# Attention with a top-1 mixture of experts on one core: second operands of VectorE in PSUM, late weight splits on ScalarE and VectorE, early loads regrouped

## The chip, the core and the metric

The kernel runs on one core of one Trainium2 chip. Time is device time in microseconds (us) of one execution; lower is better. The kernel before took 995.2 us (median of three runs, 991.33 to 996.54). A core has five engines that run beside each other and wait for each other by semaphores: TensorE (PE, its weight loads PEld), VectorE (DVE), ScalarE (ACT), GpSimd (POOL) and SyncE (SP, which here only issues transfers). Each works through its own instructions in order, so an instruction that waits holds all that stands behind it on its engine.

## What is computed

```python
scores = scale * q @ k.T                      # 8 batches x 8 heads, 576 x 576, head size 64
thresh = max(scores, -1) - tau                # tau = 0.02
scores = where(scores >= thresh, scores, -1e9)
attn   = exp(scores - max); attn /= attn.sum(-1) + 1e-9
x      = (attn @ v), heads side by side       # 4608 tokens x 512
logits = x @ w_gate + modality_bias[modality_id]
e      = argmax(logits)                       # one of 8 experts per token
gate_w = softmax(logits)[e]
out    = gate_w * (relu(x @ w1[e]) @ w2[e])   # 512 -> 1024 -> 512, all in fp32
```

## The kernel before

Attention goes pair of heads by pair of heads (32 pairs), each pair in 9 steps of 128 query rows, 288 steps in all. A step is: `qk` (PE, four matmuls of 288 columns into two PSUM banks, L827), `soft_a` (DVE row maximum L836 and threshold L838, ACT exponential L842), `soft_b` (DVE: keep what passes the threshold, with row sums, L854), `tr` (PE transposes of the probabilities L880, ACT copies them out of PSUM, L883; a remainder of 64 columns is copied by POOL or ACT, L867 and L869). Once per pair `tr_rem` and `pv` multiply with the values (L761), `x_out` turns the result (DVE, L943) and SP stores it to `xs` in device memory. For accuracy every fp32 matmul is done as three (or two) passes over high and low parts in fp32r; the "splits" that make these parts are a cast (high) and a subtraction (low).

Keys and queries of the next pair come by SP, are turned (`turn_rows`, pairs 1 to 8, by PE; `turn`, later pairs, by DVE), split by POOL (`stack`, L727 and L729) and moved between partitions by SP (`move`).

After every fourth pair a batch is complete: `gate` computes the logits, `route` (DVE, L996 to L1029) picks each token's expert and its place in a table, POOL scatters the rows into it (L1033). `pick` then chooses an expert with enough waiting tokens for a "side slot". A slot is up to 512 tokens of one expert: POOL gathers them (L1160), they are scaled by the softmax sums (L1182, `xt`), turned by PE (L1187) and split (L1191 ACT, L1192 DVE), the expert's 16 weight chunks of 128x512 are loaded by SP and split (`wsplit`, L1219 to L1223), then the first layer (`l1`, L1239, with `hh` by ACT L1251 and `hl` by DVE L1253) and the second (`l2`, L1271, results by L1279 and L1283, scattered to `out` by POOL, L1290) run on PE. Eight side slots run beside attention and just behind it; the last of them (nb = 8) can only start when all batches are routed. Then `pick_rest` (DVE, 17 short pieces on one partition, L1060 to L1126) chooses the three slots of the tail, of 512, 512 and 320 tokens, whose tiles have a `t` in front of their names (`traw`, `tw1l`, `tw2l`, `txg`).

In the side slots POOL scales `xn` and makes both parts of every weight chunk; in the tail DVE scales `xn`, ACT makes the high parts, DVE the low part of w1, POOL that of w2.

The order in which each engine's instructions stand is made while the kernel is built: every piece of work is an `op` with an engine, an assumed duration, what it reads and writes, and a due time; `Plan.order` plays these against each other with assumed latencies (`LAT`, `NEXT`, `OVER`, and `LAND` for transfers) and writes out each engine's list. A string `SHIFTS` moves every due time by a fixed amount of its own. The four single PSUM banks (`bk`) during attention, eight behind it (`bk` and `pm`), are given out by the same planner: a `Group` holds one bank from its first use to its last.

Of the kernel before, what the change touches and what calls it, by code (L numbers as in the profile page):

```python
# [77 lines left out]
class Plan:  # L78
# [4 lines left out]
    LAND = (0.2, 1.05, 1.7, 4.5)  # L83
# [62 lines left out]
    def order(self, banks, late):  # L146
# [54 lines left out]
        def begin(e, t):  # L201
# [51 lines left out]
            for j in o.succ:  # L253
                x = ops[j]
                same = x.eng == o.eng and o.dma is None
                x.soon = max(x.soon, fin + (self.NEXT if same else self.LAT).get(o.eng, 0.0 if same else 0.04))
                x.left -= 1
                if not x.left and x.hot:
                    coming.add(j)
# [7 lines left out]
        while heap:  # L267
            t = heap[0][0]
            while heap and heap[0][0] <= t + 1e-9:
# [9 lines left out]
                else:  # L279
# [10 lines left out]
                    for j in o.succ:  # L290
                        s = ops[j]
                        same = s.eng == o.eng and o.dma is None
                        s.ready = max(s.ready, t + (self.NEXT if same else self.LAT).get(o.eng, 0.0 if same else 0.04))
# [52 lines left out]
def tile_attn_moe(  # L346
# [138 lines left out]

    def load(out, in_, rd=(), wr=(), us=1.0, due=None, eng="SP"):
        q_ = {"SP": nc.sync, "ACT": nc.scalar, "POOL": nc.gpsimd}[eng]
        op(eng, 0.6, lambda: q_.dma_start(out=out, in_=in_), rd, list(wr) or [out], dma=us, due=due)
# [15 lines left out]
    vr2 = tiles(glob, 2, [P, 2, D], F32, "vr")  # L504
# [8 lines left out]
    pos2 = tiles(glob, 2, [P, NT + 1, NE], F32, "pos")  # L513
# [44 lines left out]
    def begin():  # L558
        op("DVE", 0.1, lambda: nc.vector.memset(warm, 0.0), wr=[warm])
        op("DVE", 0.1, lambda: nc.vector.memset(zero, 0.0), wr=[zero])  # L560
        def part(z, s, x, eng):
            load(first[z][s].t.rearrange("p (c x d) -> p c x d", c=NC, x=2)[:, :, x, :],
                 (k, q)[z][0, s, 0:SA, :].rearrange("(c p) d -> p c d", c=NC), wr=[(first[z][s], x)], us=0.4, eng=eng)
# [54 lines left out]
    def late_constants():  # L618
# [15 lines left out]
        mid_i = bi.t[:, 0:2 * B * NT].bitcast(I32).rearrange("p (b t two) -> p b t two", b=B, t=NT)  # L634
        mid_v = mid.bitcast(I32).rearrange("(b s two) -> b s two", s=S, two=2)
# [7 lines left out]
        def f():  # L643
            nc.vector.tensor_copy(out=mid_f[:, 1, :], in_=mid_i.rearrange("p b t two -> p (b t) two")[:, :, 0])
            nc.vector.tensor_scalar(out=mid_f[:, 0, :], in0=mid_f[:, 1, :], scalar1=0.0, scalar2=None,
                                    op0=ALU.is_equal)
        op("DVE", 0.8, f, [(bi, b) for b in range(B + 1)], [bf])
        for m, (t, key) in enumerate(((bias_t, bias_t), (bias_u, bu))):
            op("DVE", 0.45, lambda m=m, t=t: nc.vector.tensor_tensor(
                out=t, in0=mb_b[:, m:m + 1, :].to_broadcast(shp),  # L650
                in1=mid_f[:, m, :].unsqueeze(2).to_broadcast(shp), op=ALU.mult), [bx, bf], [key])
        op("DVE", 0.45, lambda: nc.vector.tensor_tensor(out=bias_t, in0=bias_t, in1=bias_u, op=ALU.add),
           [bias_t, bu], [bias_t])
        for b, xs_ in ((bx, [bx]), (bi, [(bi, b) for b in range(B + 1)])):
# [22 lines left out]
    def load_rows(p):  # L677
# [225 lines left out]
    def pv(p):  # L903
        vt, vr = vm2[p % 2], vr2[p % 2]
# [34 lines left out]
    def x_out(p):  # L939
# [6 lines left out]
        for a in range(KC):  # L946
# [3 lines left out]
                 src.rearrange("i k p r -> i k (p r)"), rd=[src], wr=[("xs", b, h, a)], us=0.6)  # L950
# [36 lines left out]
    def counted(nb):  # L987
        return pos2[(nb - 1) % 2][:, NT, :] if nb else creg

    def route(b):  # L990
# [3 lines left out]

        def f1():
            V.tensor_reduce(out=lt, in_=lg.rearrange("p c h e -> p c e h"), axis=AX.X, op=ALU.add)  # L996
            V.tensor_reduce(out=mx, in_=lt, axis=AX.X, op=ALU.max)
            V.tensor_tensor(out=lt, in0=lt, in1=mx.unsqueeze(2).to_broadcast(shp_t), op=ALU.subtract)

        def f2():  # L1000
            V.scalar_tensor_tensor(out=fe, in0=lt, scalar=0.0, in1=iota_m.unsqueeze(1).to_broadcast(shp_t),
                                   op0=ALU.is_ge, op1=ALU.mult)
            V.tensor_reduce(out=mn, in_=fe, axis=AX.X, op=ALU.min)
            V.tensor_tensor(out=oh[:, 0:NT, :], in0=iota_x, in1=mn.unsqueeze(2).to_broadcast(shp_t), op=ALU.is_equal)
        op("DVE", 1.35, f1, [lg], [lt, mx])
# [12 lines left out]
        def f4():  # L1018
            rkv = g.t[:, 0:(NT + 1) * NE].rearrange("p (t e) -> p t e", e=NE)
            V.tensor_tensor(out=pos, in0=rkv, in1=counted(b).unsqueeze(1).to_broadcast([P, NT + 1, NE]), op=ALU.add)  # L1020
            V.tensor_tensor(out=pos[:, 0:NT, :], in0=pos[:, 0:NT, :], in1=oh[:, 0:NT, :], op=ALU.mult)
            V.tensor_reduce(out=posf, in_=pos[:, 0:NT, :], axis=AX.X, op=ALU.add)
            V.memset(posf[0:P - R, NC:NT], float(TROWS))
            V.tensor_copy(out=posi, in_=posf)
        op("DVE", 1.0, f4, [g, counted(b), oh], [pos, posf, posi])
# [537 lines left out]
```

## Time and profile before

| | |
|---|---|
| runs | 991.33, 995.2, 996.54 us |
| the profiled execution | 1002.75 us, span from first to last instruction 1000.9 us |
| PE busy | 961.2 us (96%) |
| DVE busy | 747.2 us (75%) |
| ACT busy | 614.3 us (61%) |
| POOL busy | 593.8 us (59%) |
| mean granted TensorE clock | 0.988 |
| last attention step (L854) begins | 757.6 us |

Busy time is from the start of an instruction to its end, so it holds the time in which an instruction stands and waits for a resource inside the engine. PE's matmuls overlap, and their ends are modelled. [...]

### The profile page before, as it was taken

How to read it: one execution, taken by the hardware profiler on the slowest of the kernel's cores; microseconds unless marked ns; L12 is line 12 of the kernel's file. 1: busy time of each engine (PE TensorE's matmuls, PEld its weight loads, DVE VectorE, ACT ScalarE, POOL GpSimd, SP SyncE). 2: the span in 40 equal slices, each digit the busy share in tenths (PEclk: the TensorE clock that was granted, in tenths of full speed). 3: DMA queues.
4: the chain of work that ended last, by engine and by line, in shares of the span. 5: the costliest groups of instructions: out<-in, count | busy, mean ns of one | idle time of the engine just before them, and what ended most of it. 6: DMA issues, size and time to landing. Idle time of an engine off the chain costs nothing.

```text
span 1000.9 us, 19578 instructions
## 1 busy us (share of the span) xinstructions
PE 961.2 (96%) x6304; PEld 768.8 (77%) x6304; DVE 747.2 (75%) x1792; ACT 614.3 (61%) x1256; POOL 593.8 (59%) x746
## 2 busy tenths in 40 slices
PE   7999999989999999999899999999999989899997
PEld 6776677768787877778789778877887866688886
DVE  6898888878788979878878888879785574625242
ACT  6777678667767776767577668766764233143431
POOL 3533686487378645737667575538964879823241
PEclk9999999999999999999999999999999989999999
DMA  7888989888879996897679786778753376333410
GB/s 162 167 192 183 196 189 191 169 204 185 182 140 194 191 193 128 185 183 167 148 158 200 178 171 147 179 142 186 190 136 87 97 199 200 116 104 103 142 63 28
DMA packets 310448, 159.58 MB, mean 159 GB/s; under 512 B 235902, under 2 KB 281982, under 8 KB 308416
## 3 DMA queue, kind: packets, MB, share of 16 engines
q1 hardware_dynamic: 301024, 138.64, 64.3%
q0 software_dynamic: 7200, 19.07, 6.2%
q8 instruction: 52, 0.85, 0.4%
q10 hardware_dynamic: 2112, 0.52, 0.2%
q14 instruction: 60, 0.49, 0.2%
HBM read 85.98 MB, written 20.73 MB: 107 GB/s over the span
## 4 chain that ended last, share of the span: by engine, by line
PE 48%; DVE 5%; issue 3%; POOL 2%; ACT 1%; another core or an unknown queue 0%; POOLq 0%; ACTq 0%; DVEq 0%
PE bk L1239 11%; PE bk L1271 11%; PE bk L761 7%; PE s L827 7%; PE bk L880 5%; PE pm L1271 3%; PE pm L1239 1%; PE bk L1187 1%; DVE pr L854 1%; DVE nm L836 1%; DVE xn L1182 1%; DVE le L1090 1%; PE bk L893 1%; POOL out_dram L1290 0%; PE bk L961 0%
## 5 line engine op out<-in xcount | busy, mean ns | idle before, releaser
L842 ACT ACTIVATE e<-s,nm 128x576 f32<-128x576 f32 x288 | 213.9, 746 | 73.6 <-DVE nm L836 67.9
L854 DVE SCALAR_TENSOR_TENSOR pr<-s,nm,e 128x576 f32<-128x576 f32 x288 | 231.3, 812 | 28.8 <-ACT e L842 10.2
L836 DVE TENSOR_REDUCE nm<-s 128x1 f32<-128x576 f32 x288 | 214.8, 749 | 30.7 <-PE s L827 25.3
L827 PE MATMUL s<-km,q 128*128 128x288 f32 x1024 | 190.9, 313 | 7.0 <-DVE pr L854 5.0
L883 ACT COPY ptm<-bk 128x512 f32<-128x512 f32 x256 | 146.3, 592 | 45.3 <-PE bk L880 37.0
L827 PEld LDWEIGHTS s<-km,q 128*128 128x128 f32 x1024 | 147.5, 189 | 34.4 <-DVE pr L854 14.0
L880 PE MATMUL bk<-ident,pr 128*128 128x128 f32 x1152 | 166.4, 275 | 1.4 <-DVE hl L1253 1.4
L880 PEld LDWEIGHTS bk<-ident,pr 128*128 128x128 f32 x1152 | 136.6, 141 | 19.1 <-issue 2.9
L761 PE MATMUL bk<-ptm,v_m 128*64 128x256 f32 (+1 forms) x1024 | 139.7, 417 | 2.3 <-ACT ptr L900 2.3
L761 PEld LDWEIGHTS bk<-ptm,v_m 128*64 128x64 f32 x1024 | 69.2, 138 | 53.6 <-issue 11.1
L1253 DVE SCALAR_TENSOR_TENSOR hl<-bk,hh 128x512 fp32r<-128x512 f32 (+3 forms) x78 | 45.9, 591 | 64.3 <-ACT hh L1251 64.1
L1239 PE MATMUL bk<-xh,w1h 128*128 128x512 f32 (+2 forms) x240 | 89.7, 374 | 0.2
L729 POOL TENSOR_TENSOR q<-kqt,q 128x576 fp32r<-128x576 f32 x62 | 88.0, 1423 | 2.3
L1271 PE MATMUL bk<-w2h,hh 128*128 128x512 f32 x200 | 84.7, 423 | 0.0
L1239 PE MATMUL bk<-xh,w1l 128*128 128x512 f32 (+2 forms) x240 | 83.8, 349 | 0.4 <-POOL w1l L1223 0.4
L1223 POOL TENSOR_TENSOR w1l<-raw,w1h 128x512 fp32r<-128x512 f32 x64 | 82.3, 1288 | 2.9
L1239 PE MATMUL bk<-xl,w1h 128*128 128x512 f32 (+2 forms) x240 | 83.6, 348 | 0.0
L1223 POOL TENSOR_TENSOR w2l<-raw,w2h 128x512 fp32r<-128x512 f32 x64 | 81.9, 1284 | 2.2
L1271 PE MATMUL bk<-w2l,hh 128*128 128x512 f32 x200 | 79.5, 398 | 2.0 <-POOL w2l L1223 2.0
L727 POOL CAST q<-kqt 128x576 fp32r<-128x576 f32 x62 | 41.0, 668 | 65.0 <-PE s L827 36.7
L1271 PE MATMUL bk<-w2h,hl 128*128 128x512 f32 x200 | 79.1, 396 | 0.0
L1290 POOL DMA_INDIRECT out_dram<-y,tb x37 | 38.2, 1034 | 61.8 <-DVE y L1283 46.1
(226 smaller groups left out, 1784.7 us busy)
## 6 DMA issues: line engine op xcount, KB each, us to landing
raw<-in_moe_w_dram SPq DMA_DIRECT2D x128, 256.0 KB
km<-q SPq DMA_DIRECT2D x60, 288.0 KB
q<-q SPq DMA_DIRECT2D x30, 576.0 KB
nk<-km SPq DMA_DIRECT2D x97, 144.0 KB
traw<-in_moe_w_dram SPq DMA_DIRECT2D x48, 256.0 KB
xs<-xq SPq DMA_DIRECT2D x64, 144.0 KB
v_m<-in_v_dram SPq DMA_DIRECT2D x64, 128.0 KB
kq<-in_q_dram SPq DMA_DIRECT2D x46, 144.0 KB
```

Source lines behind the costliest of these rows:

```text
L729: op("POOL", 1.425, lambda s=s: nc.gpsimd.tensor_tensor(out=q2[:, 1, s], in0=kqt[:, s], in1=f32(q2[:, 0, s]), op=ALU.subtract), [kqt[:, s] ...
L761: nc.tensor.matmul(out=o, lhsT=lhsT, rhs=rhs, start=start, stop=stop, skip_group_check=True)
L827: nc.tensor.matmul(out=g.t[:, hf, 0:SH], lhsT=a, rhs=x, start=(z == 0), stop=(z == len(passes) - 1))
L836: op("DVE", 0.757, lambda: nc.vector.tensor_reduce(out=nm[:, 0, x:x + 1], in_=g.t[:, :, 0:SH], axis=AX.XY, op=ALU.max, negate=True), [g], ...
L842: op("ACT", 0.747, lambda: nc.scalar.activation(out=e, in_=g.t[:, :, 0:SH], func=AF.Exp, bias=nm[:, 0, x:x + 1]), [g, nm[:, 0, x:x + 1]], ...
L854: op("DVE", 0.826, lambda: nc.vector.scalar_tensor_tensor(out=pr.rearrange("p (a x) -> p a x", a=2), in0=g.t[:, :, 0:SH], scalar=nm[:, 1, ...
L880: op("PE", 0.44, lambda: [nc.tensor.transpose(out=g.t[:, kc * P:(kc + 1) * P], in_=pr[:, kc * P:(kc + 1) * P], identity=ident) for kc in r ...
L883: op("ACT", 0.583, lambda: nc.scalar.copy(out=o, in_=g.t.rearrange("a (k p) -> a k p", p=P)), [g], [o])
L1223: op("DVE" if d else "POOL", 0.686 if d else 1.29, lambda: (nc.vector if d else nc.gpsimd).tensor_tensor(out=lo.t, in0=raw.t, in1=f32(hi.t ...
L1239: nc.tensor.matmul(out=g.t[:, 0:WT], lhsT=a.t[:, cs], rhs=x.t[:, c, 0:WT], start=(c == 0 and y == 0), stop=(c == KC - 1 and y == 2))
L1253: op("DVE", 0.1 + 0.58 * WT / 512, lambda: nc.vector.scalar_tensor_tensor(out=hl.t[:, 0:WT], in0=g.t[:, 0:WT], scalar=0.0, in1=f32(hh.t[:, ...
L1271: nc.tensor.matmul(out=g.t, lhsT=a.t[:, ts], rhs=w.t, start=(y == 0 and i == 0), stop=(y == F2 - 1 and i == 2))
```

## The change

- `route` and `pick_rest` keep their intermediate values in a PSUM bank, so that of two tensor operands of a DVE instruction one lies in PSUM; the slots whose `xn` DVE scales get the softmax sums copied into a PSUM bank by ACT first. Some instructions are split or added for this.
- From 2 us behind the planned end of attention on (`OWN`), and in the last side slot, ACT makes the high part and DVE the low part of every weight chunk, w2 of the tail included; the last side slot's `xn` is scaled by DVE.
- Values of pairs 0 to 8 come with one transfer for both heads, four rows of device memory behind each other per partition; the keys of these pairs are laid out in the same order. The 64 remaining rows of the values of two pairs come together (`load_vr`), into one buffer of four heads in place of two buffers of two.
- The modality words come by POOL, five transfers of 4-byte words in place of nine by SP of 8-byte words, and the bias is made from them by POOL.
- The planner's assumed durations of transfers change, a wait of SP for a landing costs 0.7 more, and `SHIFTS` is another.

```diff
-    LAND = (0.2, 1.05, 1.7, 4.5)
+    LAND = (0.0, 1.0, 1.95, 4.9)
+    WAKE = 0.7
...
-        for b in range(B):
-            load(mid_i[:, b, 0:NC, :], mid_v[b, 0:SA, :].rearrange("(c p) two -> p c two", c=NC), wr=[(bi, b)], us=0.4)
-        load(mid_i[:, :, NC, :], mid_v[:, S - P:S, :].rearrange("b p two -> p b two"), wr=[(bi, B)], us=0.7)
+        for t, o in enumerate([*range(0, SA, P), S - P]):
+            load(mid_i[:, :, t], mid_v[:, o:o + P].rearrange("b p -> p b"), wr=[(bi, t)], us=0.5, eng="POOL")
...
-            nc.vector.tensor_copy(out=mid_f[:, 1, :], in_=mid_i.rearrange("p b t two -> p (b t) two")[:, :, 0])
+            nc.gpsimd.tensor_copy(out=mid_f[:, 1, :], in_=mid_i.rearrange("p b t -> p (b t)"))
...
         for s in range(2):
-            load(t[:, s], sv[s, 0:SA, :].rearrange("(c p) d -> p c d", c=NC), us=0.6)
-            load(r[s * R:(s + 1) * R], sv[:, SA:S, :].rearrange("s r d -> r s d"), us=0.2)
+            if p >= ROWS:
+                load(t[:, s], sv[s, 0:SA, :].rearrange("(c p) d -> p c d", c=NC), us=0.6)
+            elif s == 0:
+                load(t.rearrange("p s c d -> p s (c d)"), sv[:, 0:SA, :].rearrange("s (p c) d -> p s (c d)", c=NC), us=1.05)
+
+    def load_vr(p):
+        b, j = p // NPAIR, p % NPAIR
+        if p % 2 == 0:
+            for s in range(2):
+                load(vr4[s * R:(s + 1) * R], v[b, 2 * j:2 * j + 4, SA:S, :].rearrange("s r d -> r s d"), us=0.3)
...
-            V.tensor_reduce(out=mx, in_=lt, axis=AX.X, op=ALU.max)
-            V.tensor_tensor(out=lt, in0=lt, in1=mx.unsqueeze(2).to_broadcast(shp_t), op=ALU.subtract)
+            V.tensor_reduce(out=one(48), in_=lt, axis=AX.X, op=ALU.max)
+            V.tensor_tensor(out=part(64, NT), in0=lt, in1=one(48).unsqueeze(2).to_broadcast(shp_t), op=ALU.is_ge)
+            V.tensor_tensor(out=lt, in0=lt, in1=one(48).unsqueeze(2).to_broadcast(shp_t), op=ALU.subtract)
...
-        cum = fin["pool"].tile([1, 3, NE], F32, name="cum", bufs=1)
+        cum = room(3, NE)
...
+    OWN = tm(NSTEP) + 2
...
+                if xt_eng and t == 0:
+                    box["r"] = gr = Group()
+                    op("ACT", 0.25, lambda: nc.scalar.copy(
+                        out=gr.t[:, 0:TT * H].rearrange("p (t h) -> p t h", h=H), in_=tb.t[:, 0:TT, 2:TC].bitcast(F32)),
+                       late + [tb], [gr], due=plan.due - 2)
...
-                if xt_eng:
+                d = xt_eng or plan.due > OWN
+                if d:
                     op("ACT", 0.62, lambda: nc.scalar.copy(out=hi.t, in_=raw.t), late + [raw], [hi])
                 else:
                     op("POOL", 0.613, lambda: nc.gpsimd.tensor_copy(out=hi.t, in_=raw.t), [raw], [hi])
-                d = xt_eng and which == 1
                 op("DVE" if d else "POOL", 0.686 if d else 1.29, lambda: (nc.vector if d else nc.gpsimd).tensor_tensor(
                     out=lo.t, in0=raw.t, in1=f32(hi.t), op=ALU.subtract), late + [raw, hi], [lo])
...
-        for t, f in slot(z, lambda cells=cells: cells["c"], nb * S, w, rings, False, [pk_i[z]], hold=hold)(t0, span, OPEN):
+        for t, f in slot(z, lambda cells=cells: cells["c"], nb * S, w, rings, nb == B, [pk_i[z]], hold=hold)(t0, span, OPEN):
```

`part`, `one` and `room` are slices of the PSUM bank that the planner gives to `route` and to `pick_rest`.

On DVE, in the middle of `pick_rest`, there stood before (`cum`, `off`, `le` are small tiles of one partition, `hl` is the low part of a first layer's result):

```order
L1253 SCALAR_TENSOR_TENSOR hl_110<-bk_79,hh_106 128x512
L1085 TENSOR_TENSOR off<-off,ns 1x24
L1086 TENSOR_TENSOR off<-off,cum 1x24
L1090 TENSOR_TENSOR le<-ij,cum 1x88 x3
L1094 TENSOR_REDUCE ej<-le 1x33
L1098 TENSOR_SCALAR em<-ej 1x33
```

and now:

```order
L1299 SCALAR_TENSOR_TENSOR hl_110<-bk_80,hh_106 128x512
L1269 TENSOR_TENSOR w1l_90<-raw_81,w1h_87 128x512
L1115 TENSOR_TENSOR cum_t<-bk_78,tri 1x64
L1116 TENSOR_REDUCE bk_78<-cum_t 1x8
L1118 TENSOR_TENSOR off<-off,bk_78 1x24
L1120 TENSOR_TENSOR bk_78<-off,bk_78 1x24
L1124 TENSOR_TENSOR le<-ij,bk_78 1x88 x3
L1299 SCALAR_TENSOR_TENSOR hl_111<-bk_79,hh_107 128x512
```

`cum` has become a slice of a PSUM bank, and the low parts of weight chunks (`w1l`) stand between the pieces.

On POOL, where the tail's first rows are gathered (`txg`), there stood before:

```order
L1221 CAST w1h_87<-raw_84 128x512
L1223 TENSOR_TENSOR tw2l_9075<-traw_9055,tw2h_9067 128x512
L1223 TENSOR_TENSOR w1l_90<-raw_84,w1h_87 128x512
L1290 DMA out_dram<-y_118,tb_121 4608x512
L1221 CAST w2h_93<-raw_83 128x512
L1223 TENSOR_TENSOR tw2l_9077<-traw_9057,tw2h_9069 128x512
L1223 TENSOR_TENSOR w2l_97<-raw_83,w2h_93 128x512
L1223 TENSOR_TENSOR tw2l_9078<-traw_9058,tw2h_9070 128x512
L1221 CAST w1h_85<-raw_81 128x512
L1160 DMA txg_9083<-xs,tb_119 128x512
```

and now:

```order
L1197 DMA xg_100<-xs,tb_122 128x512
L1336 DMA out_dram<-y_117,tb_121 4608x512
L1336 DMA out_dram<-y_118,tb_121 4608x512
L1336 DMA out_dram<-y_117,tb_121 4608x512
L1461 TENSOR_LOAD more_i
L1336 DMA out_dram<-y_118,tb_121 4608x512
L1197 DMA txg_9026<-xs,tb_119 128x512
L1197 DMA txg_9024<-xs,tb_119 128x512
L1197 DMA txg_9025<-xs,tb_119 128x512
L1197 DMA txg_9027<-xs,tb_119 128x512
```

All casts and subtractions of weights have left this place of POOL; in all, 25 chunks of the side slots and the 24 `tw2l` have gone to ACT and DVE.

On POOL at the start, ahead of the first split of a query tile (`q`), there stood before:

```order
L597 IOTA th_lo 1x72
L620 COPY nxt<-creg 1x8
L624 MEMSET oh 128x8
L656 MEMSET xg_101 128x512
L625 MEMSET l 128x5
L660 MEMSET y_115 128x370
L660 MEMSET y_115 128x37
L621 COPY iota_x<-iota_m 128x40
L623 MEMSET iota_x 64x8
L727 CAST q_163<-kqt 128x576 x2
```

and now:

```order
L493 DMA xg_100<-in_moe_modality_id_dram 128x8x1
L628 MEMSET l 128x5
L623 COPY nxt<-creg 1x8
L493 DMA xg_100<-in_moe_modality_id_dram 128x8x1
L624 COPY iota_x<-iota_m 128x40
L658 MEMSET xg_101 128x512
L626 MEMSET iota_x 64x8
L493 DMA xg_100<-in_moe_modality_id_dram 128x8x1 x2
L878 COPY rp<-pr_177 128x64
L738 CAST q_162<-kqt 128x576 x2
```

The five modality transfers (one stands just ahead of this piece) have come in front of the first split of queries.

## Rows read from the trace of the kernel before

**Rows 1.** Busy time by stage: stretch, length, PE, PEld, DVE, ACT, POOL (count), clock, DMA share, GB/s
```profile
0.00:85.00 85.00, 76.69 (x585) 59.64 (x585) 70.28 (x181) 59.48 (x110) 34.16 (x93) 1.00 0.81 175
85.00:757.60 672.60, 656.73 (x4650) 525.59 (x4649) 567.69 (x1422) 480.33 (x1012) 430.49 (x511) 0.99 0.81 174
757.60:875.00 117.40, 108.27 (x507) 84.15 (x507) 65.52 (x117) 31.03 (x57) 91.61 (x97) 0.96 0.50 143
875.00:994.50 119.50, 119.50 (x566) 99.42 (x564) 43.00 (x73) 43.45 (x78) 35.87 (x46) 1.00 0.30 91
```

**Rows 2.** Waits of PE from 757.6 to 875 us: total us, times, longest
```profile
PE bk L1187 <- DVE xn L1182: 3.3, 1, 3.3
PE pm L1271 <- DVE hl L1253: 3.1, 1, 3.1
PE bk L1271 <- POOL w2l L1223: 2.0, 3, 0.8
```

**Rows 3.** The stretches behind the two long waits, columns as in Rows 1
```profile
802.90:809.70 6.80, 5.71 (x15) 4.55 (x16) 5.30 (x22) 0.59 (x1) 2.95 (x5) 0.50 0.22 56
854.10:857.50 3.40, 2.91 (x9) 2.52 (x10) 2.79 (x3) 0.59 (x1) 3.21 (x5) 0.50 0.37 105
```

**Rows 4.** Timeline of DVE between 796 and 867 us: start, us, instruction, idle before
```profile
796.42 5.63 DVE L1090 TENSOR_TENSOR le<-ij,cum 1x88 f32<-1x88 f32 x3
...
803.26 0.67 DVE L1253 SCALAR_TENSOR_TENSOR hl<-pm,hh 128x512 fp32r<-128x512 f32 x1
...
849.18 5.35 DVE L1182 TENSOR_TENSOR xn<-txg,tb 128x256 f32<-128x256 f32 x2 [0.48 <-PE bk L1187]
...
854.46 0.68 DVE L1192 TENSOR_TENSOR txl<-bk,txh 128x512 fp32r<-128x512 f32 x1
...
866.85 0.75 DVE L1182 TENSOR_TENSOR xn<-txg,tb 128x256 f32<-128x256 f32 x2
```

**Rows 5.** Timeline of POOL at 866 us
```profile
866.54 1.02 POOL L1290 DMA_INDIRECT out_dram<-y,tb  x1 [2.88 <-DVE y L1283]
```

**Rows 6.** POOL from 757.6 to 875 us, line 1223 alone, then line 1221 alone
```profile
757.60:875.00 117.40, 43.47 (x34) 0.96 0.50 143
757.60:875.00 117.40, 16.61 (x26) 0.96 0.50 143
```

**Rows 7.** Groups by line: count, busy us, mean ns, idle before
```profile
L1219 ACT CAST tw2h<-traw 128x512 fp32r<-128x512 f32 x24 | 14.7, 620 | 19.3 <-PE pm L1271 12.7 <-DMA traw<-in_moe_w_dram 2.6 <-PE bk L1271 2.5
```

**Rows 8.** Groups of DVE in the routing of a batch, columns as in Rows 7
```profile
L998 DVE TENSOR_TENSOR l<-l,lmx 128x40 f32<-128x40 f32 x8 | 5.7, 708 | 0.3
L1020 DVE TENSOR_TENSOR pos<-bk,pos 128x48 f32<-128x48 f32 x7 | 1.4, 205 | 1.9 <-PE bk L761 1.9
```

**Rows 9.** Line 998 alone: shortest, median, longest in ns
```profile
L998 DVE TENSOR_TENSOR l<-l,lmx x8: 199/299/2100, 101.4 to 773.5; 128x40 f32<-128x40 f32 x8
```

**Rows 10.** Timeline of DVE, and of PE, where the bias is made
```profile
46.87 1.35 DVE L644 CAST y<-xg 128x40 f32<-128x40 int32 x1 [0.73 <-DMA xg<-in_moe_modality_id_dram]
...
50.23 0.80 PE L827 MATMUL s<-km,q 128*128 128x288 f32 x4 [1.31 <-DVE pr L854]
...
54.56 0.49 DVE L649 TENSOR_TENSOR bias_t<-xg,y 128x320 f32<-128x320 f32 x1
```

**Rows 11.** Timeline of POOL at the start
```profile
1.59 0.74 POOL L488 DMA_DIRECT2D tau_b<-in_tau_dram  x1 [0.15 <-issue]
...
15.30 1.27 POOL L727 CAST q<-kqt 128x576 fp32r<-128x576 f32 x2 [9.34 <-ACT kqt L695]
```

**Rows 12.** SP: two issues of modality words; then what SP waited for
```profile
32.61 2.38 SPq L488 DMA_DIRECT2D xg<-in_moe_modality_id_dram  x2
...
SPq L488 <- PE bk L761: 22.7, 10, 8.9
```

**Rows 13.** Waits of PE from 0 to 757.6 us: total us, times, longest
```profile
PE bk L1187 <- POOL xn L1182: 3.4, 1, 3.4
PE bk L761 <- ACT ptr L900: 2.3, 1, 2.3
```

More of the change, by code (lines that the diff above doesn't have):

```diff
@@ L255, in begin @@
                 same = x.eng == o.eng and o.dma is None
-                x.soon = max(x.soon, fin + (self.NEXT if same else self.LAT).get(o.eng, 0.0 if same else 0.04))
+                x.soon = max(x.soon, fin + (self.NEXT if same else self.LAT).get(o.eng, 0.0 if same else 0.04)
+                                    + (self.WAKE if o.dma is not None and x.eng == "SP" else 0.0))
                 x.left -= 1
@@ L292, in order @@
                         same = s.eng == o.eng and o.dma is None
[L293 removed]
+                        s.ready = max(s.ready, t + (self.NEXT if same else self.LAT).get(o.eng, 0.0 if same else 0.04)
+                                        + (self.WAKE if o.dma is not None and s.eng == "SP" else 0.0))
                         s.n -= 1
@@ L1058, in pick_rest, with room @@
     def pick_rest():
-        left = fin["pool"].tile([1, NE], F32, name="left", bufs=1)
-        nc.vector.tensor_tensor(out=left, in0=counted(B)[0:1, :], in1=nxt, op=ALU.subtract)
+        at_, taken = fin["ps"], [0]
+        def room(*shape):
+            n = 1
+            for x in shape:
+                n *= x
+            taken[0] += n
+            t = at_[0:1, taken[0] - n:taken[0]]
+            if len(shape) == 2:
+                return t.rearrange("o (a b) -> o a b", b=shape[1])
+            if len(shape) == 3:
+                return t.rearrange("o (a b c) -> o a b c", b=shape[1], c=shape[2])
+            return t
+        nx, left = room(NE), room(NE)
+        nc.vector.tensor_reduce(out=nx, in_=nxt.unsqueeze(2), axis=AX.X, op=ALU.add)
+        nc.vector.tensor_tensor(out=left, in0=counted(B)[0:1, :], in1=nx, op=ALU.subtract)
         done = fin["pool"].tile([1, NE], F32, name="done", bufs=1)
-        nc.vector.tensor_tensor(out=done, in0=nxt, in1=creg[0:1, :], op=ALU.subtract)
+        nc.vector.tensor_tensor(out=done, in0=nx, in1=creg[0:1, :], op=ALU.subtract)
         yield
@@ L1085, in pick_rest @@
         nc.vector.tensor_tensor(out=off, in0=off, in1=ns, op=ALU.add)
-        nc.vector.tensor_tensor(out=off, in0=off, in1=cum, op=ALU.subtract)
+        offp = room(3, NE)
+        nc.vector.tensor_tensor(out=offp, in0=off, in1=cum, op=ALU.subtract)
         SHP = [1, MAXC, NE]
@@ L1401, in finish, with step @@
         plan.ops[-1].deps |= {i for i in range(len(plan.ops) - 1) if plan.ops[i].att}
-        steps = pick_rest()
+        steps, gp = pick_rest(), Group()
+        def step():
+            fin["ps"] = gp.t
+            next(steps, None)
         for us in [0.6] + [0.7] * 3 + [0.8] + [0.6] * 3 + [0.9, 0.5, 0.9, 0.6, 0.6, 0.9, 0.7, 1.4, 0.7]:
-            op("DVE", us, lambda: next(steps, None), ["fin", counted(B)[0:1], nxt, creg, cnt], [cnt, "si"])
+            op("DVE", us, step, ["fin", counted(B)[0:1], nxt, creg, cnt], [cnt, gp, "si"])
         for b in [tail["xg"].next() for _ in range(4)]:
```

243 lines of the change are left out of this document (127 added, 116 removed).

## The prediction

> **What bounds the kernel now.** I read the busy times by stage first, then the waits of PE in the stage that loses most, then the timeline of the engine that those waits name. The stages [rows 1]: behind the start, attention with side slots (85 to 757.6 us) keeps PE busy for 656.73 of 672.60 us, and the tail (875 to 994.5) for all of its 119.50. Between them, from the last attention step to 875 us, PE is idle for 117.40 - 108.27 = 9.1 us although only matmuls of experts are left, and the granted clock is 0.96. PE does nearly all of the work that remains there, so what it loses in this stage is lost at the end of the span too. In the first 85 us PE is idle for 8.3 us; no side slot exists yet, and the steps go at VectorE's pace (70.28 of 85 us busy).
>
> PE's waits between 757.6 and 875 us are few and long [rows 2]: 3.3 us for a scaled tile `xn`, 3.1 us for a low part `hl`, both from DVE, and 2.0 us in three waits for low parts of w2 from POOL. [...] Idle time and clock together make 9.1 + 5.1 = 14.2 us.
>
> Why DVE is late stands in its timeline [rows 4]. The `hl` that PE waits for runs in 0.67 us, but three instructions of 88 elements on one partition stood before it for 5.63 us. A pair of `xn` takes 5.35 us at 849 us and 0.75 us at 867 us. The difference is POOL: at 866.54 it only issues a transfer [rows 5], while earlier it works through weight chunks without a pause; it is busy for 91.61 of 117.40 us [rows 1], 43.47 of them with subtractions and 16.61 with casts [rows 6]. The slow DVE instructions read both operands from SBUF. Beside the same POOL work, `txl`, which reads one operand from PSUM, takes 0.68 us for 512 elements [rows 4]. So the stage is bound by POOL twice: by its own late chunks, and because it holds up DVE.
>
> **The change part by part.** The sum is made against the profiled execution's own 1002.75 us (span 1000.9); that run lies 7.55 us above the median of the runs, 995.2, and I carry the difference in us over to the median.
>
> *Late splits and `xn` to ACT and DVE.* In this stage POOL makes 34 subtractions and 26 casts [rows 6]. By the order 25 chunks and the 8 early `tw2l` go, 33 of the 34 and 25 of the 26: 42.2 + 16.0 = 58.2 us off POOL, which leaves 33.4 us in 117.4. DVE gets 33 subtractions at about 0.68 (`txl`, the nearest row) and 8 `xn` at half of 0.75: 22.4 + 3.0 = 25.4 us, which even with today's stalls left in makes 65.52 + 25.4 = 90.9 of 117.4 us. ACT gets 25 casts at 0.620 [rows 7], 15.5 us on top of 31.03. In the tail DVE gets 16 more `tw2l` (10.9 us on 43.00 of 119.5), so PE should stay full there. No engine but PE is then near its limit between 757.6 and 994.5 us, and the 14.2 us should go. What is late next would be a cast on ACT in front of an `hh`, or a subtraction on DVE in front of an `hl`: 0.6 to 0.7 us at a time, under the length of a chunk's work on PE. I leave 1.2 us for that and take 13. Bounds: 6.4 us (the two long waits alone, no clock) and 14.2.
>
> *`pick_rest` in PSUM.* The three `le` now read `cum` from PSUM, so they should no longer stand behind POOL. This is the same 3.1 us wait, counted above; either edit alone would remove it. The copies of softmax sums to PSUM cost ACT four short instructions, hidden by its idle time.
>
> *`route` in PSUM.* One of its instructions takes 708 ns on average [rows 8] and 199 at best [rows 9]: 8 x 0.51 = 4.1 us of DVE time, less about as many added instructions at 0.2 us, 1.6 us. PE is 98% busy in that stage [rows 1], so I take 0; bounds -2.5 and +1.6.
>
> [...]
>
> *Bias by POOL, words by POOL's queue.* Off DVE go 1.35 us and four instructions of about 0.49, 3.3 us, and 0.73 us in which DVE waited for the words; PE was idle for 1.31 us just behind [rows 10]. In this stage DVE sets the pace, so nearly all of it counts: bounds 1.3 and 4.0, I take 3. On POOL five transfers of 1024 words now stand ahead of the first cast of queries, where POOL was idle for 9.34 us; a transfer of 128 words took it 0.74 [rows 11]. If the price goes by instructions the five take 3.7 us and are hidden; if by words, 5 x 5.9 = 29.6 us, 20 too many. I take the first, the nearest row as it stands, and keep the other as a rival. The bias work itself, five short instructions on POOL, has the slack of a stage in which POOL is busy for 34.16 of 85 us.
>
> *Loads.* SP loses nine issues of 1.19 us [rows 12], and a few of values per pair. None of PE's longer waits in attention names a load that these would bring forward, so 0 is taken, and no loss: SP gets shorter.
>
> *The new order.* By the lists of PE, the matmuls of experts stand among the same attention steps as before, to within one or two groups of three; only near neighbours change places. Of PE's waits in attention, 3.4 us for POOL and 2.3 us for ACT [rows 13] come from places where the planned order and the chip disagreed. With the clock, at 1.7 us behind each as in [rows 3], that is 9.1 us, an estimate. A new order may lose these and have others: 0, bounds -9.1 and +9.1.
>
> Sum: -13 - 3 = -16 us: 986.7 for an execution like the profiled one, **979 us** for the median.
>
> **The rivals.**
> - *More goes.* The new order also loses the two waits, and route's DVE time and the whole of the bias count: -14.2 - 4.0 - 2.5 - 9.1 = -30, 965 us. For it: transfers and SP's wake-up are planned as longer, so fewer things should come late. Against: stalls of this sort depend on single places.
> - *Half of the end.* ACT and DVE work strictly in order, and a cast that waits for its chunk holds an `hh` behind it; PE keeps waiting in smaller pieces. Then the end gives 7 and not 13: 985 us. Against: both engines are below 80% there.
> - *The order brings its own waits.* +9.1 on the forecast: 988 us.
> - *Words priced one by one on POOL.* The first query splits come 20 us late, and the steps behind them: 979 + 20 = 999 us, no change. It decides from 5.1 us a transfer on (5 x 5.1 - 9.34 = 16). Against: the one direct transfer by POOL takes 0.74 us.
> - *Slower: one buffer for the remaining rows of values.* Fifteen times SP must now wait until the pair before has been multiplied, and SP's queue stands. SP waited for such matmuls 10 times before, 22.7 us in all [rows 12], 2.27 each. If each of the fifteen reaches PE through late weight chunks, +34: 1013 us. It decides from 16 / 15 = 1.1 us each on. Against: in SP's new list the stores of `xs`, which wait for the same matmuls and more, stand within a few places behind these loads, as they did before.
>
> **How the numbers follow.** Forecast 0.56, more 0.11, half of the end 0.10, waits of the order 0.07, words 0.07, slower 0.09. The range of 964 to 992 us leaves out the words, the slower case and the lower part of the first rival. The forecast's own range is 972 to 986. A change of 0.5%, 5 us, is about what a measurement of this kernel can tell from none: faster by more (below 990) in the first three cases and most of the fourth, 0.81; within, 0.10; slower, 0.09.
>
> **What would show it.** Right: between the last L854 step and the tail no wait of PE over 1 us and a granted clock near 1.00; the three `le` under 1 us together, every pair of `xn` under 1 us; POOL below 40 us in that stage; the third pair of heads shorter by 2 to 4 us. Wrong: PE still idle for over 5 us in that stage with ACT or DVE named; POOL's transfers of words over 2 us each and its first query cast later than 16 us; SP waiting for matmuls of L761 (now L772) far above 22.7 us; or attention ending more than 5 us later than 757.6.

## The result, and the profile after

| | before | after |
|---|---|---|
| median of four runs of each | 995.52 us | 982.37 us |
| lowest and highest | 991.33, 996.54 | 979.59, 983.71 |
| ratio after / before | | 0.9872, 95% interval 0.9837 to 0.9908 |
| the profiled execution | 1002.75 us | 982.43 us |
| last attention step begins | 757.6 us | 748.4 us |
| from there to the end of PE's work | 236.9 us | 222.2 us |
| from the end of PE's work to the end of the span | 6.4 us | 10.1 us |

The kernel is 13.2 us faster; 979 us was forecast, in a range of 964 to 992. The same stages as in [rows 1], and as a fifth row what lies behind PE's last matmul, in the trace of after (columns as there):

```profile
0.00:85.00 85.00, 79.88 (x591) 61.98 (x592) 70.23 (x183) 60.89 (x113) 44.09 (x106) 0.96 0.87 185
85.00:748.40 663.40, 650.75 (x4637) 521.31 (x4637) 566.62 (x1430) 477.50 (x1012) 424.65 (x507) 0.99 0.82 174
748.40:865.30 116.90, 116.90 (x570) 93.79 (x569) 69.71 (x169) 48.77 (x93) 34.17 (x34) 1.00 0.54 163
865.30:970.60 105.30, 105.30 (x506) 88.06 (x504) 47.24 (x81) 38.13 (x69) 14.80 (x28) 1.00 0.28 87
970.60:980.70 10.10, 0.02 (x1) 0.00 (x0) 0.75 (x1) 0.00 (x0) 0.93 (x1) 0.71 0.10 30
```

In the third row PE is busy for all of 116.90 us at a clock of 1.00, where it stood for 9.1 us at 0.96 before [rows 1]: PE has no wait at all between the last step and the tail, so nothing answers to [rows 2] and [rows 3]. POOL has fallen from 91.61 to 34.17 us. The timeline of VectorE in that stage (start, us, instruction):

```profile
788.34 0.55 DVE L1124 TENSOR_TENSOR le<-ij,bk 1x88 f32<-1x88 f32 x3
788.81 0.67 DVE L1299 SCALAR_TENSOR_TENSOR hl<-bk,hh 128x512 fp32r<-128x512 f32 x1
...
841.63 0.75 DVE L1228 TENSOR_TENSOR xn<-txg,bk 128x256 f32<-128x256 f32 x2 [1.08 <-PE bk L1233]
```

Against [rows 4], the three `le` take 0.55 us in place of 5.63, and the pair of `xn` 0.75 in place of 5.35. These are signs that the prediction named, and so is the third pair of heads, which from its first L854 (now L865) to that of the next pair took 16.9 us in place of 19.0.

Elsewhere three things differ from what was forecast. At the start, PE's idle time in the first 85 us fell from 8.3 to 5.1 us, but a stretch at half clock, 0.50 granted, stands there now. In attention a stall has appeared that before did not have. And the end of the span comes 3.7 us later behind PE's last matmul. First PE's waits up to 748.4 us (total us, times, longest), then the two stretches behind the longest of them (columns as in [rows 1]):

```profile
PE s L838 <- DVE pr L865: 6.6, 7, 4.6
PE bk L1233 <- POOL xn L1228: 3.9, 4, 1.8
PE bk L779 <- DMA raw<-in_k_dram: 1.6, 1, 1.6
```

```profile
694.90:701.70 6.80, 4.97 (x21) 4.84 (x22) 5.15 (x13) 4.53 (x10) 2.74 (x3) 0.50 0.18 44
8.80:15.60 6.80, 6.78 (x31) 5.38 (x32) 5.24 (x15) 3.29 (x10) 1.88 (x4) 0.50 1.32 143
```

At the start the clock column needs care: it counts the time ahead of the trace's first clock entry as 1.00. That entry comes at 11.0 us in the trace of before, at 5.4 us in that of after, and at 5.2 us in that of e5 (below), which starts with the same work as before. The same twelve matmuls, in before and then in e5 (timeline of PE):

```profile
7.05 2.79 PE L768 MATMUL bk<-ident,raw 128*128 128x128 f32 x12 [1.74 <-DMA raw<-in_q_dram]
7.08 1.50 PE L768 MATMUL bk<-ident,raw 128*128 128x128 f32 x12 [1.77 <-DMA raw<-in_q_dram]
```

So before too ran slowly at its start, although [rows 1] has 1.00 there; up to 11.2 us its matmuls took 1.8 us longer than those of e5.

The 4.6 us wait is for a `pr` that came late because `pick`, the choice of the seventh side slot's expert, stood on VectorE for nearly 7 us ahead of the steps' work. Its timeline, and below it that of POOL:

```profile
685.98 3.55 DVE L1062 TENSOR_TENSOR pk<-pos,nxt 1x8 f32<-1x8 f32 x1
689.57 2.01 DVE L1063 SCALAR_TENSOR_TENSOR pk<-pk,iota_m 1x8 f32<-1x8 f32 x1
691.61 0.15 DVE L1064 TENSOR_REDUCE pk<-pk 1x1 f32<-1x8 f32 x1
691.80 1.12 DVE L1065 SCALAR_TENSOR_TENSOR pk<-iota_m,pk,nxt 1x8 f32<-1x8 f32 x1
```

```profile
685.33 1.18 POOL L1268 CAST w1h<-raw 128x512 fp32r<-128x512 f32 x2
686.46 2.50 POOL L1269 TENSOR_TENSOR w1l<-raw,w1h 128x512 fp32r<-128x512 f32 x2
688.91 0.60 POOL L1268 CAST w2h<-raw 128x512 fp32r<-128x512 f32 x1
689.46 0.28 POOL L760 CAST qb<-q 64x128 fp32r<-64x128 f32 x1
```

Eight elements take 3.55 us, while the same instruction has a median of 150 ns over the eight picks. It is the hold-up of [rows 4] again, at a place that the change left as it was: L1062, L1063 and L1065 take both tensor operands from SBUF, and POOL splits weights without a pause. The reduction between them, with one operand, takes 0.15 us. L1062 waited through several of POOL's instructions on end: the rest of a cast, two subtractions (2.50 us) and another cast, with whose end at 689.5 us it ends.

To compare kernels I add up, for each trace, PE's idle time and half of the time that its clock entries have at 0.50, an estimate of what the clock took: 85 us to the last step 21.0 us before and 16.1 after; behind it 14.2 and 0.

### The profile page after: what moved, and what is told of

Its sections match the earlier page's. It is cut to its first block, busy times and chain, and to the rows that moved or that the text cites. A ratio compares the mean times of both kernels' runs of the same rounds, so it can differ in the third digit from the quotient of the medians.

```text
span 980.7 us, 19559 instructions
## 1 busy us (share of the span) xinstructions
PE 952.9 (97%) x6298; PEld 765.1 (78%) x6298; DVE 754.6 (77%) x1862; ACT 625.3 (64%) x1285; POOL 518.6 (53%) x674
## 3 DMA queue, kind: packets, MB, share of 16 engines
q0 software_dynamic: 7360, 19.09, 6.2%
## 4 chain that ended last, share of the span: by engine, by line
PE 71%; DVE 6%; issue 3%; DMA 2%; POOL 2%; ACT 2%; SPq 0%; DVEq 0%; POOLq 0%; ACTq 0%
PE bk L1285 17%; PE bk L1317 15%; PE s L838 12%; PE bk L772 11%; PE bk L891 8%; PE pm L1317 3%; DVE pr L865 2%; PE pm L1285 1%; PE bk L1233 1%; PE bk L972 1%; PE bk L904 1%; DMA tb<-tab 1%; DVE nm L847 1%; ACT e L853 1%; DMA xg<-xs,tb 1%
## 5 line engine op out<-in xcount | busy, mean ns | idle before, releaser
L865 DVE SCALAR_TENSOR_TENSOR pr<-s,nm,e 128x576 f32<-128x576 f32 x288 | 232.1, 813 | 27.1 <-ACT e L853 15.9
L838 PE MATMUL s<-km,q 128*128 128x288 f32 x1024 | 192.6, 315 | 7.3 <-DVE pr L865 6.6
L838 PEld LDWEIGHTS s<-km,q 128*128 128x128 f32 x1024 | 146.8, 190 | 37.7 <-DVE pr L865 19.1
L772 PE MATMUL bk<-ptm,v_m 128*64 128x320 f32 (+1 forms) x1024 | 136.7, 411 | 0.0
L1317 PE MATMUL bk<-w2h,hh 128*128 128x512 f32 x188 | 79.1, 421 | 0.0
L1297 ACT ACTIVATE hh<-bk 128x512 fp32r<-128x512 f32 (+3 forms) x82 | 42.9, 526 | 54.9 <-PE bk L1285 54.2
L880 ACT COPY rp<-pr 128x64 f32<-128x64 f32 x234 | 56.7, 253 | 28.9 <-DVE pr L865 27.1
L1317 PE MATMUL bk<-w2h,hl 128*128 128x512 f32 x188 | 74.0, 394 | 0.0
L1317 PE MATMUL bk<-w2l,hh 128*128 128x512 f32 x188 | 73.9, 393 | 0.0
L1299 DVE SCALAR_TENSOR_TENSOR hl<-bk,hh 128x512 fp32r<-128x512 f32 (+3 forms) x82 | 48.1, 591 | 31.2 <-ACT hh L1297 30.5
```

What stands on the lines that cost most here:

```text
L772: nc.tensor.matmul(out=o, lhsT=lhsT, rhs=rhs, start=start, stop=stop, skip_group_check=True)
L838: nc.tensor.matmul(out=g.t[:, hf, 0:SH], lhsT=a, rhs=x, start=(z == 0), stop=(z == len(passes) - 1))
L865: op("DVE", 0.826, lambda: nc.vector.scalar_tensor_tensor(out=pr.rearrange("p (a x) -> p a x", a=2), in0=g.t[:, :, 0:SH], scalar=nm[:, 1, ...
L880: op("ACT", 0.248, lambda: nc.scalar.copy(out=o, in_=i), [i], [o])
L1299: op("DVE", 0.1 + 0.58 * WT / 512, lambda: nc.vector.scalar_tensor_tensor(out=hl.t[:, 0:WT], in0=g.t[:, 0:WT], scalar=0.0, in1=f32(hh.t[:, ...
L1317: nc.tensor.matmul(out=g.t, lhsT=a.t[:, ts], rhs=w.t, start=(y == 0 and i == 0), stop=(y == F2 - 1 and i == 2))
```

## The experiments

Ratios are to the kernel before, run on the same chip; 0.0010 is 1 us. Where no other is named, an experiment is built on the changed kernel with its planned order of every engine kept, so that only the edit differs; an instruction that changes its engine keeps its place among the others.

**e1_splits_pool: late weight splits on GpSimd again.**

```diff
-  ACT: hi <- raw              DVE: lo <- raw - hi      (late side chunks; tail w2: lo)
+  POOL: hi <- raw             POOL: lo <- raw - hi     (tail w2: hi stays on ACT)
```

> The changed kernel in its own order, but the late weight splits run on GpSimd again (both parts in the side slots, the low part of w2 in the tail); second operands stay in PSUM. Theory A (the prediction's): a busy GpSimd costs PE mostly by holding up VectorE instructions whose two operands both lie in SBUF, and those are gone; only GpSimd's own late chunks come back, 2.0 us of waits and up to as much of the lower clock: 982 + 2 to 4 = 984 to 986 us, le near 0.23 us each, xn near 0.42. Theory B (GpSimd's own load is the whole of it): all of the 14 us comes back, 996 us.

Measured: 993.16 us, 0.9987 (0.9972 to 1.0002). Theory A is wrong here, by 7 us. `le` and `xn` stayed short (228 and 415 ns at the median), but PE now waited for POOL (waits of PE from 748.4 us to 880 us, then the stage):

```profile
PE pm L1287 <- POOL w1h L1266: 3.2, 2, 2.5
PE pm L1287 <- POOL w1l L1271: 2.3, 3, 1.1
PE bk L1319 <- POOL w2l L1271: 1.3, 1, 1.3
```

```profile
748.40:865.30 116.90, 109.43 (x521) 84.93 (x520) 50.73 (x130) 31.52 (x62) 89.19 (x91) 0.99 0.52 152
```

POOL is at 89.19 of 116.90 us again. Operands in PSUM free VectorE, but they do not make POOL's own chunks earlier.

**e2_operands_sbuf: operands of the end back in SBUF.**

```diff
-        at_, taken = fin["ps"], [0]
+        at_, taken = fin["pool"].tile([1, 512], F32, name="room", bufs=1), [0]
...
-                if xt_eng:
-                    r_ = lambda tb, gr=box["r"]: gr.t[:, t * H:(t + 1) * H]
```

> The changed kernel in its own order, but pick_rest works in SBUF and the late xn read the softmax sums from SBUF, as before; the late splits stay on ScalarE and VectorE. Theory A: with GpSimd nearly idle there, two operands in SBUF cost nothing, 982 us, the three le under 1 us together. Rival C (two operands in SBUF are slow by themselves): the 3.1 us and 3.3 us waits come back with the lower clock, 982 + 6 to 11 = 988 to 993 us.

Measured: 981.25 us, 0.9861 (0.9838 to 0.9883), as theory A expects. With two operands in SBUF, but little work on POOL, the first row of `le` (shortest, median, longest in ns) is:

```profile
L1124 DVE TENSOR_TENSOR le<-ij,room x3: 231/231/232, 787.3 to 787.7; 1x88 f32<-1x88 f32 x3
```

**e3_both_undone: both edits.** The two diffs above together.

> Both edits of the end undone at once, in the changed kernel's own order. Theory A: the two edits each cover the hold-up, so only without both does it come back: 982 + 14 = 996 us, le over 1 us each, xn pairs of several us. If the cost were the sum of the two single runs, theory A is wrong.

Measured: 996.32 us, 1.0017 (1.0005 to 1.0029): 14 us above the changed kernel, as expected, but e1 alone already had 11 of them. The hold-up is back on VectorE:

```profile
787.82 1.07 DVE L1124 TENSOR_TENSOR le<-ij,room 1x88 f32<-1x88 f32 x3
...
790.69 1.91 DVE L1132 TENSOR_SCALAR room<-room 1x33 f32<-1x33 f32 x1
```

So in this order of work the operands are worth 3 us (e3 against e1) while POOL is busy, and nothing when it is not (e2 against after).

**e4_pick_psum: `pick` with second operands in PSUM.**

```diff
+            n_, d_, c_, a = [g.t[0:1, NE * i:NE * i + NE] for i in range(4)]
+            nc.vector.tensor_reduce(out=n_, in_=nxt.unsqueeze(2), axis=AX.X, op=ALU.add)
-        nc.vector.tensor_tensor(out=a, in0=counted(nb)[0:1, :], in1=nxt, op=ALU.subtract)
+        nc.vector.tensor_tensor(out=d_, in0=counted(nb)[0:1, :], in1=n_, op=ALU.subtract)
```

> The changed kernel in its own order, but three of the eight picks of an expert, the seventh among them, also take their second operands from PSUM (one more short reduction each). In the changed kernel's trace the seventh took 7.9 us on VectorE (3.55, 2.01 and 1.12 us for instructions of 8 elements) beside weight splits of GpSimd, and PE then stood 4.64 us and ran 6.8 us at half clock. Theory A: the stall goes, 982 - 8 = 974 us, the seventh pick under 1.6 us. Rival: PE waits there for something else behind the pick (the transpose L954, the next row maximum), and the time stays at 980 to 982 us.

Measured: 975.23 us, 0.9806 (0.9787 to 0.9825); theory A. Of the waits of PE behind 680 us one of 0.6 us is left, and from 15.3 us to the last matmul the clock is 1.00. One instruction of the pick was still held, a cast from SBUF to SBUF (timeline of VectorE):

```profile
685.11 0.16 DVE L1066 TENSOR_TENSOR bk<-pos,bk 1x8 f32<-1x8 f32 x1
...
686.44 2.06 DVE L1076 CAST pk_i<-pk 1x2 int32<-1x2 f32 x1
```

**e5_before_splits: the kernel before, its own order, late splits on ScalarE and VectorE.**

```diff
-                    op("POOL", ..., lambda: nc.gpsimd.tensor_copy(out=hi.t, in_=raw.t), [raw], [hi])
+                    op("POOL", ..., lambda own=plan.due > OWN or last: nc.scalar.copy(out=hi.t, in_=raw.t) if own
+                       else nc.gpsimd.tensor_copy(out=hi.t, in_=raw.t), [raw], [hi])
```

and the subtraction on VectorE in the same way; the planner goes on counting both as POOL's.

> The kernel before, in its own order; the only edit is that the late weight splits (all chunks planned behind 2 us after the end of attention, the last side slot's, and the tail's w2) run on ScalarE (high part) and VectorE (low part). Second operands stay in SBUF, the last side slot's xn stays on GpSimd. Theory A, mended by the first runs (GpSimd's own late chunks are the larger part, and with GpSimd free two operands in SBUF cost nothing): the 14.2 us of idle time and half clock between the last attention step and the tail go, 994 - 14 = 980 us, le under 0.3 us each. Rival D (the gain of the end needs the new order as well): half of it, 985 to 990 us.

Measured: 0.9869 (0.9839 to 0.9898), on a slower chip (986.55 us against 1001.38 of before); on a scale of 994 us that is 981, theory A. One of the change's edits alone gives as much as the whole change. Only the sign for `le` was not met: one of the three still took 1.37 us. The stage behind the last step (columns as in [rows 1]):

```profile
755.00:870.00 115.00, 114.43 (x558) 90.93 (x557) 66.77 (x158) 47.80 (x90) 37.87 (x40) 1.00 0.54 159
```

**e6_pick_words: e4, and the words by GpSimd 14 us later.**

```diff
-        order = the planned order
+        order = body with the five word transfers behind the first splits of queries, and
+                what is made of them just ahead of the first product with the bias
```

> As e4_pick_psum, and GpSimd issues the five transfers of modality words, and what depends on them, only behind the first splits of queries (about 22 us in place of 5 to 9 us). Theory E (the words' 5120 small packets get in the way of the first keys and queries): PE's two waits for raw at 5.7 and 7.5 us (1.8 us) and the half clock behind them (6.8 us, 3.4 lost) go, 975 - 4 = 971 us. Rival: the first loads are late for their own reasons (their new order of rows), and the time stays at 975 us.

Measured: 0.9802 (0.9774 to 0.9830), no gain over e4. PE's waits for `raw` and the 6.8 us at half clock stayed where they were: theory E is wrong. Its 5120 packets, one for each word, were an estimate that the profile doesn't show: in the trace of after q0, the queue of GpSimd's transfers, has 7360 packets, 160 more than in that of before. The first pair of heads, with the words now among its splits, took 18.9 us in place of 16.8.

**e7_bias_dve: the bias on VectorE.**

```diff
-            nc.gpsimd.tensor_copy(out=mid_f[:, 1, :], in_=mid_i.rearrange("p b t -> p (b t)"))
+            nc.vector.tensor_copy(out=mid_f[:, 1, :], in_=mid_i.rearrange("p b t -> p (b t)"))
```

and the four instructions behind it.

> The changed kernel in its own order, but the bias is made on VectorE again (the five instructions from the cast of the words to the sum); the words still come by GpSimd's queue. By the prediction's term: 982 + 3 = 985 us. Rival: the stage has cover for them, 982 us.

Measured: 0.9862 (0.9832 to 0.9893). The ratio shows no loss, but its interval is 3 us to either side, as wide as the term. The trace shows a loss of about half the term: the second pair of heads, where the bias is made here, took 19.3 us, against 18.0 in after and in five others that make it on POOL (e1 to e4 and e6), and in the first 85 us PE stood 1.5 us longer than in after, nearly all of it for VectorE (the stage, columns as in [rows 1], and PE's largest wait in it, which in after is 1.1 us in two):

```profile
0.00:85.00 85.00, 78.39 (x580) 60.38 (x581) 70.51 (x182) 59.81 (x111) 40.69 (x98) 0.96 0.84 182
```

```profile
PE s L838 <- DVE pr L865: 2.5, 4, 0.9
```

**e8_before_again: a second trace of before.** No edit.

> The kernel before once more, for a second trace. The first trace was of an execution of 1002.75 us, 7 us above its runs. If its stalls belong to the kernel, this trace shows the same waits of PE and stretches of half clock at 994 to 996 us and the surplus lies elsewhere; if some were of that execution alone, they are missing here: about 7 us less of idle time and half clock.

Measured: 998.23 us, with a median of 1001.38 on that chip. The waits of PE behind the last step are those of [rows 2]:

```profile
PE bk L1187 <- DVE xn L1182: 3.3, 1, 3.3
PE pm L1271 <- DVE hl L1253: 3.1, 1, 3.1
PE bk L1271 <- POOL w2l L1223: 2.0, 3, 0.8
```

They belong to the kernel. Of the stretches at half clock several lie elsewhere (6.8 us at 110 us where the first trace had 3.4 us at 130; none at 499; one behind the last step in place of two), and 85 us to the last step lost 18.2 us in place of 21.0: there, an execution differs from the next by some 3 us.

**e9_words_sp: e6, with the words issued by SyncE.**

```diff
-            load(mid_i[:, :, t], ..., wr=[(bi, t)], us=0.5, eng="POOL")
+            op("POOL", 1.0, lambda t=t, o=o: nc.sync.dma_start(out=mid_i[:, :, t], ...), (), [(bi, t)], dma=0.5)
```

> As e6_pick_words, but the five transfers of modality words are issued by SyncE (one behind each of five of its loads from about 25 us on) and none by GpSimd. In every trace with GpSimd's word transfers the program's end has a GpSimd semaphore increment of 1.10 us and a drain of 3.75 us, and in every trace without them 0.38 and 0.80 us. Theory F (these transfers leave something that GpSimd's queue has to clear at the end): 0.38 and 0.80 us again, end of PE to end of span 6.4 in place of 9.8 us, 0.9805 x before - 3.6 us, so a ratio of 0.977. Rival: the length of the drain comes from elsewhere in the changed program, and the ratio stays at 0.980 to 0.981.

Measured: 0.9817 (0.9793 to 0.9840). Theory F is right that the transfers are the cause: semaphore increment and drain of GpSimd take 0.38 and 0.81 us, and the stretch behind PE's last matmul is 6.40 us again (columns as in [rows 1]):

```profile
966.10:972.50 6.40, 0.02 (x1) 0.00 (x0) 0.75 (x1) 0.00 (x0) 1.68 (x2) 0.72 0.18 58
```

But the time did not fall, since PE waited elsewhere for a transfer that the words had pushed back on SyncE (waits of PE between 30 and 60 us):

```profile
PE s L843 <- DMA qb<-q: 3.3, 1, 3.3
```

**e10_words_sp_warm: e9, and 16 more matmuls on zeros at the start.**

```diff
-                            x.fn = make(g, int((gap - self.REST) * self.SHARE / 0.056))
+                            x.fn = make(g, int((gap - self.REST) * self.SHARE / 0.056) + (16 if end < 8 else 0))
```

> As e9_words_sp, with 16 more matmuls on zeros ahead of the first key tile, so that PE doesn't stand still from 5.8 to 7.5 us. Theory G (the half clock at 8 to 15 us follows that pause): the stretch goes, 3.4 us less than e9. Rival: the clock falls all the same, or the steps behind go at VectorE's pace, and the time is e9's.

Measured: 971.92 us, 0.9772 (0.9753 to 0.9792), 4.3 us less than e9, about the number of theory G. But the profile doesn't bear its mechanism out: a stretch at half clock still came at 11.8 us, and e9's trace had none there without the extra matmuls; the two profiled executions have the same span (972.6 and 972.5 us). Where the 4.3 us come from stays open.

What makes the clock fall in the first 17 us stays open too. The clock entries have no stretch at 0.50 there in e5, e9 and e12, 3.4 us in e10, and 6.8 us in after, e1, e2, e4, e6, e7 and e11. In before, e8 and e3 the first entry comes only at 11.0, 11.0 and 17.3 us, and the matmuls ahead of it go at the pace of 0.50: the first eight L838 of e3 took 2.69 us, as in after at 0.50 (2.68), against 1.63 in e9 at 1.00. Yet e3 starts with the same work as after, and e5 and e11 start with that of before.

**e11_before_rest_psum: the kernel before, its own order, `pick_rest` in PSUM.**

```diff
+            fin["ps"] = banks[0]
-            op("DVE", us, lambda: next(steps, None), ["fin", ...], [cnt, "si"])
+            op("DVE", us, step, ["fin", ...], [cnt, "si"])
```

with the changed kernel's `pick_rest`.

> The kernel before, in its own order; the only edit is that pick_rest works in a PSUM bank. GpSimd keeps all its late chunks and the tail's xn read both operands from SBUF. The prediction's step (either edit alone removes the wait for hl): le under 0.3 us each, and before - 6.5 us (3.1 of waiting, 3.4 of half clock), a ratio of 0.9935. Rival H (GpSimd's chunks are late right behind, as when the splits were put back on it): PE waits for GpSimd's w1l, w2l in its place, before - 0 to 3 us, 0.997 to 1.000.

Measured: 989.90 us, 0.9949 (0.9930 to 0.9968), 5.1 us of gain; 6.5 was expected and lies inside the interval. The first row of `le`, and the longest waits of PE from 755 us to 880 us:

```profile
L1107 DVE TENSOR_TENSOR le<-ij,pm x3: 226/227/234, 789.6 to 790.0; 1x88 f32<-1x88 f32 x3
```

```profile
PE bk L1205 <- DVE xn L1200: 3.3, 1, 3.3
PE bk L1289 <- POOL w2l L1241: 1.9, 3, 0.8
```

The wait for `hl` is gone without POOL having lost a chunk, and rival H is wrong; the one for `xn`, which this edit does not touch, stays.

**e12_words_sp_78us: e10, with the words at about 78 us.**

```diff
-            words behind five loads from 25 us on
+            four words behind the move of queries at 78 us, one behind the next load
```

> As e10_words_sp_warm, but SyncE issues the words at about 78 to 81 us, where it stood idle for 2.2 us, in place of 30 to 37 us, and GpSimd makes the bias behind that. In e10's trace the words pushed the transfer of qb back, and PE then waited 2.55 us for it at 43.6 us and ran 3.4 us at half clock. If that wait came from SyncE's queue, it goes: 4.2 us less than e10, a ratio of 0.973. Rival: SyncE is nowhere free in that stage and another load is late, or the bias comes late for the first routing; then the ratio stays at 0.977 or rises.

Measured: 973.97 us, 0.9788 (0.9765 to 0.9810); the rival. The wait at 43 us is gone, and another load is late (waits of PE from 60 to 100 us):

```profile
PE bk L701 <- DMA kq<-in_q_dram: 3.9, 1, 3.9
```

## Why the prediction was right, and where it was not

The sign, the place and the size of the main term were right. That the sum came out 3.4 us below the measured time is in part luck, because its other errors cancelled.

*The end, -13.* From the last step to the end of PE's work it is 14.7 us less than in the first trace of before and 13.3 less than in the second (235.5 us); e5 has -13.1 us from the splits alone, at 1001. The 1.2 us left over for new waits was not needed. The 5.1 us of clock in the 14.2 is half of the 6.80 and 3.40 us at 0.50 in [rows 3]; with the late splits moved the clock of the stage is 1.00, in after as in e5.

*"Either edit alone would remove it."* For the wait for `hl` that is so, from before's side: e11 removes it by operands, e5 by splits. Read as "either edit does the work of the end" it fails: in the new order, with operands in PSUM and the chunks on POOL, 11 of the 14 us come back (e1), as waits for POOL's chunks, which before were only the 2.0 us of [rows 2]. Why more in e1 than in e11 I cannot settle; e1's order was planned for faster splits.

*The bias, -3.* This term was too large. The bias on VectorE costs 1.3 us in e7's trace (second pair of heads). I had counted 3.3 us of VectorE as PE's because VectorE was busy for 70.28 of 85 us [rows 1]; busy for 83% leaves room, and only the 1.31 us in which PE stood for it [rows 10] were shown to be on the path, the lower bound that I had given. Pairs two and three together, in which before made the bias, became 2.2 us shorter (34.9 for 37.1); what of the other 0.9 us is the missing wait for the words, and what the new order, no run separates. The named sign, a shorter third pair, does not tell: it is 16.9 us in e7 as well.

*The clock at the start, no term.* The first step began 1.2 us later than in before. After lost 3.4 us to its half clock at 8.8 us, before 1.8 us ahead of its first clock entry, and PE's idle time in the first 85 us fell by 3.2 us.

*The new order, 0 with bounds of 9.1 either way.* The value was a balance of two terms near the bound. Without the stall at `pick`, 85 us to the last step loses 8.2 us (e4) where before lost 21.0 and 18.2; with it 16.1. So order, loads and route, which no run takes apart, gave about 10 us or more there, and 8 went back at one place. With all of the end's edits undone, order, loads, bias and route together are worth +0.17% (e3), no gain, though in an order planned for the faster splits.

*Nothing forecast, +3.7.* The end of the span behind PE's last matmul had no term at all: 10.1 us against 6.4.

*Route, 0.* L1014, with one operand in PSUM, takes 195 ns every time, where [rows 9] had 199 to 2100; the added instructions take about 0.2 us each. An operand in PSUM cost little or nothing: L1013, which reads and writes PSUM, takes 203 ns for 40 elements, against the 199 of [rows 9].

*The words on POOL.* They took 0.88 to 0.98 us each for 1024 words, where the transfer of 128 words in the same trace took 0.73, so their price goes by instructions far more than by words. The sign that I had named, the first cast of queries later than 16 us, came true all the same (17.39 us), without its cause: the first step was 1.2 us later. It was a poor sign.

*One buffer for the remaining values.* SP's waits for such matmuls fell to 7.6 us in six from the 22.7 of [rows 12].

*Carrying 7.55 us over from the profiled execution to the median.* The sum for the profiled executions was 986.7 and the one of after took 982.43; the medians differ by 13.2 and not by 16. By parts, against the first trace: -14.2 at the end, -4.9 in attention, 0.2 at the start, +3.7 behind PE is -15.2; against the second -12.6, -2.1, -0.6 and +3.7, which is -11.6. The spans differ by more, 20.2 and 15.8 us: 1.8 us of the rest is before's start ahead of its first clock entry, and 2 to 3 us stand neither as idle time nor in the clock's entries and stay open. The stalls of the end were in both traces, so they could be carried over as they stood; what an unusually slow execution has on top could not.

A faster kernel than both came out of this: e4 at 0.9806, and e10 at 0.9772. Their intervals meet, so that e10 beats e4 isn't settled.

## What to carry to other kernels

When a trace shows an engine held up by another, list every instruction of that shape in the program, not only those that stall in this execution: the change cured two groups and a third, `pick`, stalled next. Price busy time taken off an engine by the waits that end on it, not by its share: here 1.3 us and not 3. Look at what lies behind the last matmul too: a cheap transfer moved to another queue can be paid for there, here with 3.7 us.

## What the runs showed of the hardware

- Five transfers of 1024 four-byte words each by GpSimd, at 5 or at 22 us, lengthen the program's end: the records of GpSimd's sequencer there have a semaphore increment of 1.10 us and a drain of 3.75 us, against 0.38 and 0.80 without them, and the stretch behind PE's last matmul is 9.8 to 10.1 us in seven traces with them and 6.4 or 6.5 in seven without. e9 shows that the transfers are the cause. What makes the drain longer the traces do not show.
- GpSimd's hold-up of VectorE isn't confined to two tensor operands: a cast of two elements from SBUF to SBUF took 2.06 us, to 688.5 us, where a weight cast of POOL ends too (e4), a `tensor_scalar` of 33 elements 1.91 us, to 792.6 us, again with the end of a cast of POOL (e3). In after the same cast takes 0.16 us in all eight picks.
- In neither of the two places tried on SyncE's queue were five small transfers free: with them at 30 to 37 us PE waited 2.5 and 3.3 us for `qb` (e10, e9), with them at 76 to 82 us 3.9 us for `kq` (e12), waits that e4 does not have. By GpSimd they cost about 3.5 us at the end. In these runs the price of the words was about the same either way.
- The same work at the start of a program ran at different clocks from trace to trace: the first entry of the granted clock comes at 11.0, 11.0, 5.2 and 4.5 us in before, e8, e5 and e11, and of these only e11 has 6.8 us at 0.50 from 7.9 us on. The clock column counts the time ahead of the first entry as 1.00.
